# FNet with a gated linear unit: neighbouring tokens share a partition, the normalising passes walk in storage order, and the first DFT block is loaded in one piece

## The chip, the cores and the metric

One core of a Trainium2 chip runs the whole kernel. The metric is the device time of one execution in microseconds; the time before is the median of three runs. The trace and the page of the profile come from one profiled execution of the same kernel.

## The reference

All values are 32-bit floats, S = 2048 tokens, D = 512 features, F = 1792.

```python
xn = layernorm(x)                       # over the 512 features of a token
a, b = xn @ Wd_re.T, xn @ Wd_im.T       # DFT along the features
s = Ws_re @ a - Ws_im @ b               # DFT along the tokens, real part
h = sigmoid(xn @ w_gate) * (xn @ w_up)
g = silu(h @ w_down)
out = x + s * g
```

## The kernel before

**Work and engines.** The kernel does the DFT along the tokens first, then the gated unit on the transposed x, then the DFT along the features. Each matrix product is cut into 2 by 2 blocks and done with seven block products instead of eight (Strassen's scheme in Winograd's form), so VectorE forms sums of blocks (`combine`, L127), and every operand is split into a high and a low part for three passes of TensorE: ScalarE writes the high part (L118), VectorE the low one by a subtraction (L123), TensorE multiplies (`mm3`, L70). GpSimd issues the stores to scratch memory (g_part, f_raw, f_sum) and does small arithmetic of the statistics; SyncE issues all loads.

**Order.** The program is written as a list of units, each one block product, with 12 to 18 matmuls. A loop at the end (L851) goes through the units, and ahead of each one loads what the next five need, splits what the next two need, and runs what was hung on that unit with `sooner`, `amid` and `after`. No scheduler moves anything: the instructions of an engine run in the order in which this loop emits them.

**Tokens.** Tokens are cut into 4 groups of 512 (index pp or b), and each group into 4 blocks of 128 tokens, named by (e, j). Block halves j = 0 and 1 are the two halves of the 2 by 2 scheme along the tokens; e counts the two 128-row pieces that a page holds. Before, token 128 (4 pp + 2 e + j) + p lies on partition p. The page `xs[j, pp]` is [128, 2, 512]; `fetch` (L149) fills it with two transfers of 128 rows each. `seq` in `_layout` lays the two DFT matrices out on the host in the matching order, in blocks [128, 2, 512], each contiguous in memory. `c_block` names such a block, and `Load.load` (L76) fetches it with one transfer.

**Statistics.** `stats` (L156) forms mean, scale and bias of each token with VectorE (L162, L163, L168, L170) and GpSimd (L169, L171) into the tile `moments`. `normalise` (L174) applies them on ScalarE, a token for each partition. `store_moments` writes mean and scale of a group to scratch memory as m_part, [128, 2, 4].

**The normalising passes by features.** For the gated unit, x is needed with features on partitions: `x_t` holds it transposed, a page [128 features, 2, 512 tokens], tokens in their order in memory. Here mean and scale differ along the row, so `x_norm` (L425) loads m_part to every partition as `both`, [128, 128 p, 2, 4], and `step` (L431) adds the mean in one pass and multiplies by the scale in the next, in place, each one VectorE instruction over 128x1024 (L435). There are 16: 2 halves, 2 groups in each, 2 pages, 2 passes. They are hung on units at the end of the DFT along the tokens and within the gated unit.

**The startup.** `begin` (L347) warms TensorE with products of ones, then emits the first loads by hand: the two pieces of the first x page, the two halves of the first DFT block (L358), and then x pages and DFT blocks by turns. The first unit's operands are split by halves e, the DFT block's half ahead of x's (`high` L376, `low` L379, `normed` L373).

Of the kernel before, what the change touches and what calls it, by code (L numbers as in the profile page):

```python
# [8 lines left out]
F32 = mybir.dt.float32  # L9
F32R = mybir.dt.float32r  # L10
AF = mybir.ActivationFunctionType
# [3 lines left out]
P = 128  # L15
# [6 lines left out]
NT = S // 512  # L22
SB = 512
# [9 lines left out]
def fnet_glu_kernel(ctx: ExitStack, tc: tile.TileContext, x, x_t, c_re, c_im, w_h, w_gu, w_down, out):  # L33
    nc = tc.nc
# [8 lines left out]
    def page(shape, dtype=F32R):  # L43
        return pages.tile([P, *shape], dtype, name="page")

    def bank(tag):
        return banks.tile([P, 512], F32, name=tag, bufs=2 if tag == "pd" else 1)
# [7 lines left out]
    moments = const.tile([P, 4, 3, 2, 2], F32, name="moments")  # L55
    m_part = [dram.tile([P, 2, 4], F32, name=f"m_part{i}") for i in range(NT)]
# [42 lines left out]
    class Parts(Value):  # L99
# [6 lines left out]
        def begin(self):  # L106
            if self.raw is None and self.at is None:
                self.raw = self.src()
# [21 lines left out]
    units = []  # L130
# [6 lines left out]
    def after(n, f):  # L137
        extra.setdefault(n, []).append(f)

    def sooner(n, f):  # L140
        early.setdefault(n, []).append(f)
# [5 lines left out]
    xs, mvs = {}, {}  # L147

    def fetch(j, pp, es=(0, 1)):  # L149
        if (j, pp) not in xs:  # L150
            xs[j, pp] = page([2, D], F32)
        for e in es:
            i = 4 * pp + 2 * e + j
            nc.sync.dma_start(xs[j, pp][:, e, :], x[i * P : (i + 1) * P, :])

    def stats(j, pp):  # L156
        mv = stat.tile([P, 2, 2], F32, name="mv")
        rs = stat.tile([P, 2], F32, name="rs")
        mean, scale, bias = (moments[:, pp, m, :, j] for m in range(3))
        for e in range(2):  # L160
            st = stat.tile([P, 6], F32, name="st")
            nc.vector.bn_stats(st, xs[j, pp][:, e, :])  # L162
            nc.vector.bn_aggr(mv[:, e, :], st)  # L163
            if pp == j == 0:
                nc.gpsimd.tensor_scalar(rs[:, e : e + 1], mv[:, e, 1:2], EPS, None, op0=ALU.add)
                nc.gpsimd.tensor_tensor(scale[:, e : e + 1], rs[:, e : e + 1], mhalf[:, e : e + 1], op=ALU.pow)
        if pp or j:
            nc.vector.tensor_scalar(rs, mv[:, :, 1], EPS, None, op0=ALU.add)  # L168
            nc.gpsimd.tensor_tensor(scale, rs, mhalf, op=ALU.pow)  # L169
        nc.vector.tensor_scalar(mean, mv[:, :, 0], -1.0, None, op0=ALU.mult)  # L170
        nc.gpsimd.tensor_tensor(bias, mean, scale, op=ALU.mult)  # L171
        return mv

    def normalise(j, pp, d=None):  # L174
        for e in range(2):
            v = xs[j, pp][:, e, :] if d is None else a_block(d, j, pp)[:, e]
            nc.scalar.activation(v, v, AF.Identity, scale=moments[:, pp, 1, e, j : j + 1], bias=moments[:, pp, 2, e, j : j + 1])

    def store_moments(b):
        nc.gpsimd.dma_start(m_part[b], moments[:, b, 0:2].rearrange("p m e j -> p m (e j)"))  # L180


    def a_block(d, j, pp):
        return xs[j, pp][:, :, d * D // 2 : (d + 1) * D // 2]
# [130 lines left out]
    def begin_seq():  # L315
        tags = ("a", "b", "pd"), ("c", "pd", "a"), ("b", "pd", "a"), ("c", "a", "pd")
        chunks = [Chunk(t, dict(zip("abc", tags[t])), t in (1, 2)) for t in range(NT)]
        for i, k in enumerate((1, 2)):
            for pp in range(4):
                for c in chunks[:2]:  # L320
                    add(c.needs(k, pp), lambda c=c, k=k, pp=pp: c.run(k, pp))
                m = 8 * i + 2 * pp
                if m > 4:
                    sooner(m - (6, 7)[i], lambda i=i, pp=pp: fetch(i, pp))
                if m > 2:
                    sooner(m - (4, 5)[i], lambda i=i, pp=pp: stats(i, pp))
                    sooner(m - 2, units[m][0][1].get)
                    sooner(m - 2, lambda i=i, pp=pp: normalise(i, pp))
                if i:
                    after(m + 2, lambda pp=pp: store_moments(pp))  # L330
# [16 lines left out]
    def begin(chunks):  # L347
        for i, tag in enumerate(("gb", "ub", "pd", "pd")):
            idle = bank(tag)
            for _ in range((4, 4, 2, 2)[i]):  # L350
                nc.tensor.matmul(idle, ones[:, :P], ones, start=True, stop=True)
        c = chunks[0].op[1, 0]
        raw = c.loads[0]
        raw.at = page(raw.shape, F32)
        for e in range(2):
            fetch(0, 0, (e,))
        for e in range(2):
            nc.sync.dma_start(raw.at[:, e, :], raw.src[:, e, :])  # L358
        fetch(0, 1)
        for n in (1, 2):  # L360
            units[n][0][1].load()
        fetch(0, 2)
        for n in (3, 4, 5):
            units[n][0][1].load()
        a = aop[1, 0]
        both = page([2, 2, D // 2])
        a.at = both[:, 0], both[:, 1]
        c.at = page([2, SB]), page([2, SB])
        first = a_block(0, 0, 0)

        def normed(e):
            scale = moments[:, 0, 1, e, 0:1]
            nc.vector.tensor_scalar(first[:, e], first[:, e], mv[:, e, 0:1], scale, op0=SUB, op1=ALU.mult)  # L373

        def high(parts, src, e):
            nc.scalar.activation(parts[0][:, e], src[:, e], AF.Copy)  # L376

        def low(parts, src, e):
            nc.vector.tensor_tensor(parts[1][:, e], src[:, e], parts[0][:, e].bitcast(F32), op=SUB)  # L379

        mv = stats(0, 0)
        high(c.at, raw.at, 0)
        normed(0)
        high(a.at, first, 0)
        low(c.at, raw.at, 0)
        low(a.at, first, 0)
        high(c.at, raw.at, 1)
        normed(1)
        high(a.at, first, 1)
        low(c.at, raw.at, 1)  # L390
        low(a.at, first, 1)
        units[1][0][1].high()
        stats(0, 1)
        units[1][0][1].get()
        units[2][0][1].get()
        normalise(0, 1, d=0)
        aop[1, 1].get()
        for pp in range(2):
            after(4 + pp, lambda pp=pp: normalise(0, pp, d=1))
# [25 lines left out]
    def x_norm(h, b, at):  # L425

        c = 2 * h + b
        both = Load(m_part[c].rearrange("p m o -> (p m o)").partition_broadcast(P).rearrange("k (p m o) -> k p m o", m=2, o=4), [P, 2, 4])
        raw = [Load(x_t[c * 2 + j], [2, SB]) for j in range(2)]

        def step(j, m):  # L431
            v = xraw[h, j, b] = raw[j].load()
            to = v.rearrange("k i (o p) -> k i o p", o=4)
            by = both.load()[:, :, m, :].rearrange("k p o -> k o p").unsqueeze(1).to_broadcast([P, 2, 4, P])
            nc.vector.tensor_tensor(to, to, by, op=(ADD, ALU.mult)[m])  # L435

        sooner(at[0] - 5, both.load)
        for i in range(4):
            if i % 2 == 0:
                sooner(at[i] - 5, raw[i // 2].load)  # L440
            after(at[i], lambda i=i: step(*divmod(i, 2)))
# [381 lines left out]
    with tc.manual_schedule():  # L823
        chunks = begin_seq()
        n = len(units)
# [48 lines left out]
def _layout(inputs):  # L874
    import numpy as np

    def seq(c):
        c = np.asarray(c).reshape(NT, SB, 4, 2, 2, P)
        return np.ascontiguousarray(c.transpose(0, 4, 2, 5, 3, 1))

    def hid(re, im):
        w = np.stack([np.asarray(v).T.reshape(2, 2, P, 2, D // 2) for v in (im, re)])
        return np.ascontiguousarray(w.transpose(4, 1, 3, 0, 2, 5)).reshape(2, 2, P, 4, D // 2)

    def quads():
        a = np.stack([np.asarray(inputs["B_w_gate"]), np.asarray(inputs["B_w_up"])])
        a = a.reshape(2, 2, 2, P, NG, 2, P)
        a = a.transpose(4, 5, 1, 3, 0, 2, 6)
        order = [[(0, 0), (0, 1)], [(1, 1), (1, 0)]]
        return np.ascontiguousarray(  # L890
            np.stack([np.stack([a[:, i, j] for i, j in k], axis=2) for k in order], axis=1)
        ).reshape(NG, 2, P, 2, 4 * P)

    return {
        "x": np.ascontiguousarray(np.asarray(inputs["A_x"]).reshape(S, D)),
        "x_t": np.ascontiguousarray(
            np.asarray(inputs["A_x"]).reshape(NT, SB, 2, 2, P).transpose(0, 2, 4, 3, 1)
        ).reshape(2 * NT, P, 2, SB),
        "c_re": seq(inputs["A_dft_seq_re"]),
        "c_im": seq(inputs["A_dft_seq_im"]),  # L900
        "w_h": hid(inputs["A_dft_hid_re"], inputs["A_dft_hid_im"]),
        "w_gu": quads(),
        "w_down": np.ascontiguousarray(np.asarray(inputs["B_w_down"]).reshape(NG, 2, P, D).transpose(0, 2, 1, 3)),
    }
# [16 lines left out]
```

## Time and profile before

| | us |
|---|---|
| median of 3 runs (809.91 to 810.92) | 810.75 |
| the profiled execution | 810.13 |
| its span | 808.3 |
| TensorE busy | 789.9 (98%) |
| VectorE busy | 699.5 (87%) |
| ScalarE busy | 510.6 (63%) |
| GpSimd busy | 122.2 (15%) |

The clock granted to TensorE is 0.999 of the full one over the span. The DMA engines move 174.72 MB, 216 GB/s on the mean. In rows of the profile PE is TensorE's matrix work, PEld its loading of weights, DVE VectorE, ACT ScalarE, POOL GpSimd and SP SyncE; L435 is line 435 of the kernel before; `x16 | 34.2, 2138 | 0.0` reads: 16 instructions, 34.2 us busy, 2138 ns each, 0.0 us idle of the engine ahead of them. A row of the timeline gives start, length, engine, line, operation, and in brackets the idle time ahead and who ended it.

### The profile page before, as it was taken

What the parts mean: (1) busy time and instruction counts of PE and PEld (TensorE: products, weight loads), DVE (VectorE), ACT (ScalarE), POOL (GpSimd) and SP (SyncE); (2) the same over time, 40 slices, a digit from 0 to 9 for tenths busy, and PEclk for the clock granted to TensorE, in tenths of its full rate; (3) what the DMA queues carried; (4) which work ended last, traced back from release to release, by engine and by line L of the source; (5) the groups of instructions that cost most, each with busy time, mean ns of one, the idle gap of its engine ahead of it and who ended that gap; (6) DMA issues with size and microseconds to landing.
All of it is one profiled execution on the core that took longest, in us unless ns stands there. A gap on an engine that the chain in (4) does not pass through costs nothing.

```text
span 808.3 us, 9885 instructions
## 1 busy us (share of the span) xinstructions
PE 789.9 (98%) x3468; PEld 649.1 (80%) x3468; DVE 699.5 (87%) x894; ACT 510.6 (63%) x776; POOL 122.2 (15%) x162
## 2 busy tenths in 40 slices
PE   7999999999999999999998999999999999999997
PEld 5788888888878888878876887888888888888886
DVE  7898999788899999899999966869688888896957
ACT  4984654534434455676767866767577787897571
POOL 3330001001110000011211211222131121111301
PEclk9999999999999999999999999999999999999999
DMA  9964066385997336137965987799999798999996
GB/s 347 405 210 156 1 212 230 128 340 217 295 415 298 104 131 212 50 126 198 214 115 82 171 168 179 237 272 247 259 234 221 160 232 223 230 286 305 301 332 105
DMA packets 50481, 174.72 MB, mean 216 GB/s; under 512 B 5632, under 2 KB 5888, under 8 KB 50432
## 3 DMA queue, kind: packets, MB, share of 16 engines
q0 software_dynamic: 20320, 70.28, 39.6%
q1 hardware_dynamic: 30032, 103.76, 35.6%
q8 instruction: 27, 0.44, 0.2%
q14 instruction: 22, 0.18, 0.1%
q10 hardware_dynamic: 80, 0.07, 0.0%
HBM read 106.95 MB, written 70.80 MB: 220 GB/s over the span
## 4 chain that ended last, share of the span: by engine, by line
PE 59%; issue 27%; DMA 6%; DVE 4%; POOL 3%; ACT 1%; SPq 0%; POOLq 0%; DVEq 0%; ACTq 0%
PE pd L70 18%; PE ga L70 11%; PE ua L70 11%; PE uc L70 6%; PE gc L70 6%; DMA g_part<-page 4%; PE ub L70 4%; PE gb L70 4%; POOL g_part L477 2%; DVE page L127 1%; DVE page L123 1%; DMA f_raw<-page 1%; DMA page<-in_c_re_dram 1%; DVE st L162 0%; POOL f_raw L273 0%
## 5 line engine op out<-in xcount | busy, mean ns | idle before, releaser
L118 ACT ACTIVATE page<-page 128x512 fp32r<-128x512 f32 (+1 forms) x384 | 303.6, 831 | 159.8 <-DVE page L127 131.7
L123 DVE TENSOR_TENSOR page<-page 128x512 fp32r<-128x512 f32 (+1 forms) x384 | 349.3, 941 | 59.2 <-ACT page L118 57.2
L70 PE MATMUL pd<-page 128*128 128x512 f32 (+1 forms) x984 | 238.9, 387 | 1.8 <-ACT page L486 1.1
L70 PEld LDWEIGHTS pd<-page 128*128 128x128 f32 x984 | 182.9, 188 | 40.7 <-ACT page L486 1.5
L127 DVE TENSOR_TENSOR page<-page 128x1024 f32<-128x1024 f32 (+2 forms) x252 | 205.5, 836 | 3.5 <-DMA page<-in_w_gu_dram 2.7
L70 PE MATMUL ga<-page 128*128 128x512 f32 x600 | 154.2, 391 | 6.9 <-ACT page L118 2.9
L70 PE MATMUL ua<-page 128*128 128x512 f32 x600 | 153.0, 389 | 0.0
L70 PEld LDWEIGHTS ga<-page 128*128 128x128 f32 x600 | 112.1, 188 | 33.4 <-ACT page L594 4.9
L70 PEld LDWEIGHTS ua<-page 128*128 128x128 f32 x600 | 112.6, 188 | 23.5
L477 POOL DMA_DIRECT2D g_part<-page x76 | 66.4, 874 | 281.1 <-ACT page L486 160.7
L70 PE MATMUL gc<-page 128*128 128x512 f32 x384 | 98.9, 390 | 0.4 <-DVE page L123 0.3
L70 PE MATMUL uc<-page 128*128 128x512 f32 x384 | 98.4, 389 | 0.0
L486 ACT ACTIVATE page<-pd 128x512 f32<-128x512 f32 x140 | 81.4, 599 | 23.4 <-PE pd L70 16.1
L70 PEld LDWEIGHTS gc<-page 128*128 128x128 f32 x384 | 71.8, 188 | 16.3 <-DVE page L123 0.9
L70 PEld LDWEIGHTS uc<-page 128*128 128x128 f32 x384 | 72.1, 188 | 15.0
L70 PE MATMUL gb<-page 128*128 128x512 f32 x252 | 64.9, 390 | 2.0 <-DVE page L123 2.0
L70 PE MATMUL ub<-page 128*128 128x512 f32 x252 | 64.6, 389 | 0.0
L70 PEld LDWEIGHTS gb<-page 128*128 128x128 f32 x252 | 47.2, 188 | 12.2 <-DVE page L123 2.4
L70 PEld LDWEIGHTS ub<-page 128*128 128x128 f32 x252 | 47.3, 188 | 9.8
L273 POOL DMA_DIRECT2D f_raw<-page x16 | 8.7, 545 | 220.0 <-DVE page L285 147.1
L435 DVE TENSOR_TENSOR page<-page 128x1024 f32<-128x1024 f32 x16 | 34.2, 2138 | 0.0
L612 DVE TENSOR_TENSOR page<-page 128x512 f32<-128x512 f32 x28 | 19.3, 690 | 8.0 <-ACT page L609 7.1
(90 smaller groups left out, 344.4 us busy)
## 6 DMA issues: line engine op xcount, KB each, us to landing
g_part<-page POOLq DMA_DIRECT2D x84, 512.0 KB, 7.1
page<-in_c_re_dram SPq DMA_DIRECT2D x47, 512.0 KB, 7.1
page<-in_c_im_dram SPq DMA_DIRECT2D x32, 512.0 KB, 6.1
page<-f_raw SPq DMA_DIRECT2D x28, 512.0 KB, 7.7
page<-in_w_gu_dram SPq DMA_DIRECT2D x22, 512.0 KB, 6.4
f_raw<-page POOLq DMA_DIRECT2D x16, 512.0 KB, 6.2
f_sum<-page POOLq DMA_DIRECT2D x16, 512.0 KB, 7.4
page<-f_sum SPq DMA_DIRECT2D x16, 512.0 KB, 12.2
```

What stands on the lines that cost most here:

```text
L70: nc.tensor.matmul(ps, ws[w], ms[m], start=first and i == 0, stop=last and i == 2, skip_group_check=go_on)
L118: nc.scalar.activation(self.parts[0], self.raw, AF.Copy)
L123: nc.vector.tensor_tensor(lo, self.raw, hi.bitcast(F32), op=SUB)
L127: (engine or nc.vector).tensor_tensor(dst, a, b, op=op)
L273: nc.gpsimd.dma_start(f_raw[self.t][block], v)
L435: nc.vector.tensor_tensor(to, to, by, op=(ADD, ALU.mult)[m])
L477: nc.gpsimd.dma_start(g_part[i], pg, accum_op=ADD)
L486: nc.scalar.activation(pg[:, o, :], po, AF.Copy, scale=float(sign))
L612: nc.vector.tensor_mul(s[k][:, 0, :], s[k][:, 0, :], ps["u" + tag] if tag else s[k][:, 1, :])
```

## The change

Token 512 pp + 4 p + 2 j + e now lies on partition p. So a page `xs[j, pp]` takes two neighbouring rows of x for each partition, and `fetch` of a whole page is one transfer of 4 KB pieces; the first page is still fetched as two transfers, of 2 KB pieces with a step of 8 KB. `seq` lays the DFT matrices out to match, `moments` has its last two indices exchanged. In `step` the token index of a row of 512 is now 4 p + (2 j + e), so both operands are walked with the four values of a partition p innermost, which is the order in which `both` stores them: four neighbouring floats, then a gap of four to the next p. Before, p was the innermost index, with a step of 8 floats in `both`. The number, shape and place of all passes stay as they are.

In `begin`, the first DFT block is fetched by one transfer. The second unit's block goes ahead of the second x page, and one more block ahead of the third.

```diff
     def fetch(j, pp, es=(0, 1)):
         if (j, pp) not in xs:
             xs[j, pp] = page([2, D], F32)
-        for e in es:
-            i = 4 * pp + 2 * e + j
-            nc.sync.dma_start(xs[j, pp][:, e, :], x[i * P : (i + 1) * P, :])
+        rows = x[pp * SB : (pp + 1) * SB, :].rearrange("(p j e) d -> p j e d", j=2, e=2)[:, j]
+        if len(es) == 2:
+            nc.sync.dma_start(xs[j, pp], rows)
+        else:
+            nc.sync.dma_start(xs[j, pp][:, es[0], :], rows[:, es[0], :])
...
-        mean, scale, bias = (moments[:, pp, m, :, j] for m in range(3))
+        mean, scale, bias = (moments[:, pp, m, j, :] for m in range(3))
...
         c = chunks[0].op[1, 0]
         raw = c.loads[0]
-        raw.at = page(raw.shape, F32)
         for e in range(2):
             fetch(0, 0, (e,))
-        for e in range(2):
-            nc.sync.dma_start(raw.at[:, e, :], raw.src[:, e, :])
+        raw.load()
+        for n in (1,):
+            units[n][0][1].load()
         fetch(0, 1)
-        for n in (1, 2):
+        for n in (2, 3):
             units[n][0][1].load()
         fetch(0, 2)
-        for n in (3, 4, 5):
+        for n in (4, 5):
             units[n][0][1].load()
...
         def step(j, m):
             v = xraw[h, j, b] = raw[j].load()
-            to = v.rearrange("k i (o p) -> k i o p", o=4)
-            by = both.load()[:, :, m, :].rearrange("k p o -> k o p").unsqueeze(1).to_broadcast([P, 2, 4, P])
+            to = v.rearrange("k i (p o) -> k i p o", o=4)
+            by = both.load()[:, :, m, :].unsqueeze(1).to_broadcast([P, 2, P, 4])
             nc.vector.tensor_tensor(to, to, by, op=(ADD, ALU.mult)[m])
...
     def seq(c):
-        c = np.asarray(c).reshape(NT, SB, 4, 2, 2, P)
-        return np.ascontiguousarray(c.transpose(0, 4, 2, 5, 3, 1))
+        c = np.asarray(c).reshape(NT, SB, 4, P, 2, 2)
+        return np.ascontiguousarray(c.transpose(0, 4, 2, 3, 5, 1))
```

Two lines are added within `fetch`, so that lines behind it have numbers greater by two in the changed kernel: L435 there is L437, L376 is L378. Elsewhere in the code `normalise`, `store_moments` and `normed` follow the exchanged indices of `moments`.

The order of SyncE's queue at the program's start, before (in_x_dram is x, in_c_re_dram the real DFT matrix, one row of 128x512 is 256 KB):

```order
L154 DMA page<-in_x_dram 128x512 x2
L358 DMA page<-in_c_re_dram 128x512 x2
L154 DMA page<-in_x_dram 128x512 x2
L79 DMA page<-in_c_re_dram 128x1024 x2
L154 DMA page<-in_x_dram 128x512 x2
L79 DMA page<-in_c_re_dram 128x1024 x3
L154 DMA page<-in_x_dram 128x512 x4
```

and the same piece in the changed kernel:

```order
L156 DMA page<-in_x_dram 128x512 x2
L79 DMA page<-in_c_re_dram 128x1024 x2
L154 DMA page<-in_x_dram 128x1024
L79 DMA page<-in_c_re_dram 128x1024 x2
L154 DMA page<-in_x_dram 128x1024
L79 DMA page<-in_c_re_dram 128x1024 x2
L154 DMA page<-in_x_dram 128x1024 x2
```

The first DFT block and the first unit's counterpart for the second chunk now stand ahead of the second x page; each x page from there on is one transfer, and one DFT block has moved ahead of the third.

ScalarE at the program's start, before, with the semaphores that each instruction waits for (DMAHW2 and so on are lanes of SyncE's transfers, used by turns; L376 splits the first unit's operands, L118 is the next block's high part):

```order
L376 ACTIVATE page<-page 128x512 [waits DMAHW2_49]
L376 ACTIVATE page<-page 128x256 [waits DMAHW0_49,DVE_49]
L376 ACTIVATE page<-page 128x512 [waits DMAHW3_49]
L376 ACTIVATE page<-page 128x256 [waits DMAHW1_49,DVE_49]
L118 ACTIVATE page<-page 128x1024 [waits DMAHW6_49]
```

and in the changed kernel:

```order
L378 ACTIVATE page<-page 128x512 [waits DMAHW2_49]
L378 ACTIVATE page<-page 128x256 [waits DMAHW0_49,DVE_49]
L378 ACTIVATE page<-page 128x512
L378 ACTIVATE page<-page 128x256 [waits DMAHW1_49,DVE_49]
L118 ACTIVATE page<-page 128x1024 [waits DMAHW3_49]
```

The third instruction has lost its wait, since the first one's transfer brings both halves, and the second block's high part waits for the transfer right behind it. The order of instructions on ScalarE, VectorE, TensorE and GpSimd is the same in both kernels.

More of the change, by code (lines that the diff above doesn't have):

```diff
@@ L176, in normalise @@
             v = xs[j, pp][:, e, :] if d is None else a_block(d, j, pp)[:, e]
-            nc.scalar.activation(v, v, AF.Identity, scale=moments[:, pp, 1, e, j : j + 1], bias=moments[:, pp, 2, e, j : j + 1])
+            nc.scalar.activation(v, v, AF.Identity, scale=moments[:, pp, 1, j, e : e + 1], bias=moments[:, pp, 2, j, e : e + 1])
     def store_moments(b):
-        nc.gpsimd.dma_start(m_part[b], moments[:, b, 0:2].rearrange("p m e j -> p m (e j)"))
+        nc.gpsimd.dma_start(m_part[b], moments[:, b, 0:2].rearrange("p m j e -> p m (j e)"))
     def a_block(d, j, pp):
@@ L371, in normed @@
         def normed(e):
-            scale = moments[:, 0, 1, e, 0:1]
+            scale = moments[:, 0, 1, 0, e : e + 1]
             nc.vector.tensor_scalar(first[:, e], first[:, e], mv[:, e, 0:1], scale, op0=SUB, op1=ALU.mult)
```

## The prediction

> **What bounds the kernel now.** I read the page first, then TensorE's waits, then VectorE in the stretches where those waits stand. The page's line of engines:
>
> ```profile
> PE 789.9 (98%) x3468; PEld 649.1 (80%) x3468; DVE 699.5 (87%) x894; ACT 510.6 (63%) x776; POOL 122.2 (15%) x162
> ```
>
> TensorE is busy for 98% of the span, and the change gives it the same instructions. What can move is only the time it loses, and the waits of TensorE list it; behind the startup they lie in 200 to 300 and in 340 to 460 us, but for one (columns: total us, times, longest):
>
> ```profile
> PE gb L70 <- DVE page L123: 2.0, 1, 2.0
> PE gc L70 <- DVE page L123: 0.3, 1, 0.3
> ```
> ```profile
> PE ga L70 <- ACT page L594: 2.0, 3, 0.7
> PE pd L70 <- ACT page L486: 1.1, 1, 1.1
> PE pd L70 <- DVE page L572: 0.7, 1, 0.7
> ```
>
> The first group (2.3 us) names VectorE, the second (3.8 us) VectorE or ScalarE. That VectorE is the real cause there shows in the busy times by stretch (columns: length, then PE, PEld, DVE, ACT, POOL):
>
> ```profile
> 218.80:236.70 17.90, 15.89 (x71) 12.81 (x70) 17.90 (x17) 4.79 (x6) 2.87 (x5) 1.00 1.00 379
> 236.70:274.00 37.30, 37.02 (x162) 30.32 (x163) 37.25 (x29) 17.23 (x20) 2.34 (x4) 1.00 0.60 243
> 340.00:400.00 60.00, 59.43 (x262) 48.65 (x261) 58.50 (x86) 45.49 (x81) 8.27 (x11) 1.00 0.65 169
> 400.00:460.00 60.00, 56.77 (x246) 45.34 (x245) 59.45 (x82) 42.87 (x75) 10.40 (x12) 1.00 0.71 114
> ```
>
> VectorE is full: 17.90 of 17.90 us, 37.25 of 37.30, 59.45 of 60. So in these stretches, and only there, a shorter VectorE instruction is a shorter kernel. What a wait costs beyond its idle time is seen around the one at 432.62 on TensorE's timeline:
>
> ```profile
> 429.98 1.52 PE L70 MATMUL uc<-page 128*128 128x512 f32 x6
> 432.62 1.66 PE L70 MATMUL pd<-page 128*128 128x512 f32 x6 [1.12 <-ACT page L486]
> 434.12 1.52 PE L70 MATMUL gb<-page 128*128 128x512 f32 x6
> 435.48 0.84 PE L70 MATMUL ub<-page 128*128 128x512 f32 x3
> ```
>
> Undisturbed, six matmuls start 1.36 us after the six before (434.12 to 435.48). Here the steps are 2.64 and 1.50, so 1.42 us are lost where the row says 1.12: 0.30 more for each wait. The first group thus loses 2.3 + 2 x 0.3 = 2.9 us, the second 3.8 + 5 x 0.3 = 5.3 us, and 8.2 us in all is the most that a faster VectorE can return here.
>
> **The normalising passes (L435).** The groups by shape:
>
> ```profile
> L127 DVE TENSOR_TENSOR page<-page 128x1024 f32<-128x1024 f32 x92 | 112.0, 1224 | 0.0
> ...
> L435 DVE TENSOR_TENSOR page<-page 128x1024 f32<-128x1024 f32 x16 | 34.2, 2138 | 0.0
> ```
>
> Same operation, same shape, same type, yet 2138 ns against 1224. The difference is how the second operand is walked: `both` is [token p, mean or scale, 4], and the old order takes p innermost, a step of 8 floats at every element. The new order takes the 4 neighbouring floats first and hops after each four. No row of this trace walks an operand so. The bounds are 1224 (as L127, no hop) and 2138 (a hop as dear as four old steps). If a hop costs what it costs now, (2138 - 1224) / 1024 = 0.89 ns, 256 of them add 0.23 us and the pass takes 1.45. I take the end that it is nearest to, 1.22 us, so 0.9 us less for each pass, 14.6 us of VectorE's time over 16.
>
> [...]
>
> Where the passes lie decides what they are worth. The busy time of L435 alone, in the stretches between TensorE's waits:
>
> ```profile
> 216.80:236.70 19.90, 4.28 (x2) 1.00 1.00 382
> 236.70:270.00 33.30, 8.59 (x4) 1.00 0.62 254
> 340.00:354.00 14.00, 2.10 (x1) 1.00 0.10 39
> 354.00:400.00 46.00, 6.45 (x3) 1.00 0.82 208
> 400.00:422.00 22.00, 8.57 (x4) 1.00 0.72 129
> ```
>
> The waits stand at:
>
> ```profile
> 236.68 1.43 PE L70 MATMUL gb<-page 128*128 128x512 f32 x5 [2.01 <-DVE page L123]
> 269.92 1.43 PE L70 MATMUL gc<-page 128*128 128x512 f32 x5 [0.28 <-DVE page L123]
> ```
> ```profile
> 353.60 1.65 PE L70 MATMUL ga<-page 128*128 128x512 f32 x6 [0.57 <-ACT page L594]
> ```
> ```profile
> 412.13 1.65 PE L70 MATMUL ga<-page 128*128 128x512 f32 x6 [0.68 <-ACT page L594]
> ```
>
> The other three of the second group come after 412.13, the first of them at 432.62 (above). One by one: ahead of 236.68 two passes save 1.8 us of the 2.3 lost there; 0.5 stays. Four more lie ahead of 269.92, where 0.6 is lost, and all of it goes. One lies ahead of 353.60 (4 us earlier), and its 0.9 covers the 0.9 lost. Three passes up to 400 us I count at nothing: VectorE has 1.5 us of idle time in 340 to 400, so it was not the limit all along, and TensorE lost nothing between. Four lie in 400 to 422, behind which 3.8 - 0.57 = 3.2 us of idle time and 4 x 0.3 are lost, 4.4 in all; they save 3.6, and VectorE stays the limit for the remaining 0.8. ScalarE, which the rows name here, waits for VectorE itself and follows it. Sum: 1.8 + 0.6 + 0.9 + 3.6 = **6.9 us gained**.
>
> **The first block whole, and the new order of loads.** The chain of work through the startup:
>
> ```profile
> 1.65 4.17 DMA page<-in_c_re_dram
> 5.82 0.02 issue
> 5.84 0.64 ACT page L376
> ...
> 8.79 0.61 DVE st L162
> ...
> 15.51 0.61 DVE st L162
> ```
>
> ScalarE's first split starts when the first half of the block is in, at 5.82. Now it waits for both halves. SyncE's timeline has the issues of the halves and of the next block, and the DMA issues of two narrow windows how long the second half and that next block took to land:
>
> ```profile
> 1.65 0.91 SPq L358 DMA_DIRECT2D page<-in_c_re_dram  x2
> ...
> 3.55 0.91 SPq L79 DMA_DIRECT2D page<-in_c_re_dram  x2
> ```
> ```profile
> page<-in_c_re_dram SPq DMA_DIRECT2D x1, 256.0 KB, 4.4
> ```
> ```profile
> page<-in_c_re_dram SPq DMA_DIRECT2D x1, 512.0 KB, 5.6
> ```
>
> The second half, issued at some 2.1 (0.91 us for both), was in at 2.1 + 4.4 = 6.5, 0.7 us behind the first. The one transfer needs one issue instead of two, so I take 0.6 us of delay; the ends are 0 (in as soon as the half was) and 0.7. Everything on the chain follows from this split, by ScalarE's and VectorE's order, up to TensorE's last wait of the startup:
>
> ```profile
> 21.98 1.20 PE L70 MATMUL ga<-page 128*128 128x512 f32 x4 [1.41 <-ACT page L118]
> ```
>
> The next wait in its timeline is that at 236.68, so nothing in between takes a delay up. **0.6 us lost**, in full.
>
> The x load that L162 waits for moves behind a 512 KB block. The bytes up to and with it are the same as were up to and with that block, which was in at 3.55 + 5.6 = 9.15. VectorE comes to L162 at 8.79 + 0.6 = 9.4, so the move costs nothing by 0.25 us; should the slower split not come, this cover is gone and 0.35 is the price. Behind it come two blocks and the next x load, 1.5 MB; at the rate of the 2 MB moved from 1.65 to 9.15 these take 5.6 us and are in by 14.8, and L162 asks for that x at 15.51 + 0.6 = 16.1. SP's queue issues seven transfers fewer and is not the limit. Longer pieces of x and moments stored side by side I cost at nothing: neither shortens the chain above.
>
> **Sum.** 6.9 - 0.6 = 6.3 us less. The profiled execution took 810.13 us (span 808.3, 1.8 around it) and would take 803.8. The runs' median, 810.75, is 0.6 above it, so 810.75 - 6.3 = 804.45, rounded **804.5 us**.
>
> **Rivals.**
> - *B, the freed time is only half returned.* In 400 to 460 us ScalarE stands between VectorE and every wait, with 42.87 us of work in its own order. If its order holds, only the waits that name VectorE or have a pass right ahead (1.8 + 0.6 + 0.9) go, and little behind 400: 3.3 - 0.6 = 2.7 less, 808.1; with 0.7 lost at the start and the 0.6 at 269.92 not returned, 808.8. For it: the 0.8 that is left anyway. Against it: VectorE at 59.45 of 60.
> - *C, the passes stay at 2.1 us.* The change of order would then not do what it seems to, because the broadcast, not the step, is what costs. That leaves the 0.6 lost: 811.4, within 0.2% (1.6 us, about what a measurement of this kernel can tell from no change). Against it: the broadcast re-reads rows, and costs no fetch that L127 doesn't make too. [...]
> - *D, slower: short runs are dearer than single steps.* Each pass restarts its walk 256 times. Over 914 / 256 = 3.6 ns a restart, the pass gets slower. At twice that, it takes 3.05 us, the same seven passes ahead of the waits push TensorE back by 7 x 0.9 = 6.3 us, and with the startup that is 817.7. Against it: a hop at every element costs 0.89 ns now.
>
> **Chances and range.** The forecast 0.68, B 0.18, C 0.08, D 0.06. Faster by over 0.2%: the forecast and nearly all of B, 0.84; within 0.2%: C and the tail of B, 0.10; slower: D, 0.06. The range goes from all 8.2 us returned with no loss at the start (802.5) to B's far end (808.8); C and D, 0.14, and what little lies past the ends are left out.
>
> **What would show it.** L435's line (two lines further down in the changed file) at about 1.2 us and x16. TensorE's wait near 236 down from 2.0 to some 0.3, the one near 270 gone, at most one left of those from 412 to 444. The one wait of TensorE behind 460 us unchanged, as no pass lies near it. The first split some 0.6 us later than 5.84, TensorE's first real matmul and its last wait of the startup by as much. I am wrong if the passes stay above 1.5 us, if VectorE gets idle time in 400 to 460 and TensorE still waits there, or if the startup's waits grow by over a microsecond.

## The result, and the profile after

| | median us | lowest to highest | ratio to before | 95% interval |
|---|---|---|---|---|
| before (5 runs) | 810.6 | 808.49 to 810.92 | | |
| changed (5 runs) | 803.86 | 802.95 to 804.23 | 0.9921 | 0.9909 to 0.9933 |

The changed kernel is 6.7 us faster by the medians. Its profiled execution took 804.23 us with a span of 802.4, 5.9 us less than that of before; the traces are compared on this difference. The ranges of the two kernels do not meet.

The passes, in the groups by shape of the changed kernel (L437 is the former L435):

```profile
L127 DVE TENSOR_TENSOR page<-page 128x1024 f32<-128x1024 f32 x92 | 111.5, 1218 | 0.2 <-DMA page<-in_c_im_dram 0.2
...
L437 DVE TENSOR_TENSOR page<-page 128x1024 f32<-128x1024 f32 x16 | 19.5, 1217 | 0.0
```

A pass now costs what the other operations of its shape cost, 1217 ns instead of 2138: 14.7 us of VectorE's time are gone. TensorE's waits behind the startup, for 200 to 300, 340 to 460 and 460 to 800 us:

```profile
PE gb L70 <- DVE page L123: 0.4, 1, 0.4
```
```profile
PE ga L70 <- ACT page L596: 0.5, 1, 0.5
```
```profile
PE ga L70 <- ACT page L596: 0.6, 1, 0.6
```

Of 2.3 us of waits in the first stretch 0.4 are left, of 3.8 in the second 0.5. VectorE by stretch:

```profile
340.00:400.00 60.00, 60.00 (x266) 49.63 (x266) 56.47 (x87) 45.91 (x81) 9.14 (x12) 1.00 0.69 175
400.00:460.00 60.00, 59.51 (x263) 48.96 (x262) 59.45 (x87) 47.36 (x81) 10.37 (x12) 1.00 0.76 133
```

In 400 to 460 us VectorE is as full as it was (59.45), but it does 87 instructions there instead of 82, and TensorE 263 instead of 246. The startup went the other way. VectorE's first statistics, ScalarE's first split and TensorE's first real matmul, before and changed (brackets: the idle time ahead and what ended it):

```profile
3.41 0.69 DVE L162 BATCH_NORM_STATS2 st<-page 128x6 f32<-128x512 f32 x1 [2.02 <-DMA page<-in_x_dram]
...
6.83 1.26 PE L70 MATMUL ga<-page 128*128 128x512 f32 x3 [1.05 <-ACT page L376]
```
```profile
4.14 0.70 DVE L164 BATCH_NORM_STATS2 st<-page 128x6 f32<-128x512 f32 x1 [2.75 <-DMA page<-in_x_dram]
...
6.05 0.69 DVE L164 BATCH_NORM_STATS2 st<-page 128x6 f32<-128x512 f32 x1 [1.00 <-DMA page<-in_x_dram]
...
7.37 1.46 ACT L378 ACTIVATE page<-page 128x512 fp32r<-128x512 f32 x3 [5.14 <-DMA page<-in_c_re_dram]
...
8.35 1.29 PE L70 MATMUL ga<-page 128*128 128x512 f32 x3 [1.42 <-ACT page L378]
```

The split, at 7.37, starts 1.53 us later than before (5.84), not 0.6, and the x pieces, whose landing I took as unchanged, are late too: the second one at 6.05, where VectorE before never waited for it.

Since TensorE does the same matmuls in the same order in both, the time of the n-th one in the two traces shows where time went. The delay of the changed kernel is +1.52 us at the first real matmul, +1.75 behind the last wait of the startup (21.98 before), +1.71 ahead of the wait near 236 us, and -6.08 at the end of the last wait (502.78 before). Behind that it changes by no more than 0.05 us. By place:

| place (time before, us) | predicted, us | measured, us |
|---|---|---|
| startup | +0.6 | +1.71 |
| wait at 236.68 | -1.8 | -1.64 |
| wait at 269.92 | -0.6 | -0.43 |
| wait at 353.60 | -0.9 | -0.74 |
| waits from 410 to 444 | -3.6 | -3.95 |
| smaller losses near 292, 382, 496 and 502 | 0 | -1.03 |
| sum | -6.3 | -6.08 |

### The profile page after: what moved, and what is told of

Read it like the earlier page. It is cut to its first block, busy times and chain, and to the rows that moved or that the text cites. A ratio compares the mean times of both kernels' runs of the same rounds, so it can differ in the third digit from the quotient of the medians.

```text
span 802.4 us, 9870 instructions
## 1 busy us (share of the span) xinstructions
PE 790.3 (98%) x3468; PEld 651.6 (81%) x3468; DVE 685.9 (85%) x894; ACT 510.7 (64%) x776; POOL 123.0 (15%) x162
## 4 chain that ended last, share of the span: by engine, by line
PE 85%; DVE 5%; DMA 4%; issue 4%; POOL 1%; ACT 1%; SPq 0%; POOLq 0%; ACTq 0%; DVEq 0%
PE pd L70 25%; PE ga L70 15%; PE ua L70 15%; PE gc L70 10%; PE uc L70 10%; PE gb L70 5%; PE ub L70 5%; DMA g_part<-page 2%; DVE page L127 2%; DVE page L123 1%; DMA page<-in_x_dram 1%; DMA f_raw<-page 1%; POOL g_part L479 1%; ACT page L118 0%; DVE page L574 0%
## 5 line engine op out<-in xcount | busy, mean ns | idle before, releaser
L118 ACT ACTIVATE page<-page 128x512 fp32r<-128x512 f32 (+1 forms) x384 | 303.1, 829 | 148.3 <-DVE page L127 116.5
L574 DVE TENSOR_TENSOR page<-page,pd 128x512 f32<-128x512 f32 x28 | 18.5, 684 | 6.9 <-PE pd L70 6.9
```

The lines of the kernel that those rows point to most:

```text
L118: nc.scalar.activation(self.parts[0], self.raw, AF.Copy)
L574: nc.vector.tensor_add(self.part[:, o, :], self.part[:, o, :], ps)
```

## The experiments

My theory: a single-float step of 32 bytes in the second operand is what costs 0.9 us a pass; where VectorE is full, its time shows one for one at TensorE; the whole block delays the first split by 0.6 to 0.7 us. What was open after the result was the other 1.1 us of the startup. The theories are numbered in the expectation of the first run. All ratios are to the kernel before, on the same chip.

**The startup's loads alone, on the kernel before.** Edit:

```diff
-        raw.at = page(raw.shape, F32)
         for e in range(2):
             fetch(0, 0, (e,))
-        for e in range(2):
-            nc.sync.dma_start(raw.at[:, e, :], raw.src[:, e, :])
+        raw.load()
+        for n in (1,):
+            units[n][0][1].load()
         fetch(0, 1)
-        for n in (1, 2):
+        for n in (2, 3):
...
```

> The kernel before with the startup's part of the change alone: first DFT block in one transfer and the changed order of loads; tokens, x pieces and passes as before. Theory 1 (the whole block is what delays the first split): the split starts at 6.4 to 6.6 us instead of 5.84, the first real matmul 0.6 us later, the kernel 0.6 us slower (ratio 1.0007). Theory 2 (the x pieces of 2 KB with a step of 8 KB are what made the changed kernel's startup later than that): the same 0.6 us here, and the other 1.1 us of the changed kernel's 1.7 are missing. Theory 3 (the order and the single transfer cost all of it): split at 7.3 us, 1.7 us slower (ratio 1.002). Passes at 2.14 us in all three.

Measured: 811.02 us against 810.46, ratio 1.0004 (0.9993 to 1.0014), which by itself tells nothing apart. The trace does:

```profile
3.23 0.69 DVE L162 BATCH_NORM_STATS2 st<-page 128x6 f32<-128x512 f32 x1 [1.84 <-DMA page<-in_x_dram]
...
6.61 1.46 ACT L376 ACTIVATE page<-page 128x512 fp32r<-128x512 f32 x3 [4.39 <-DMA page<-in_c_re_dram]
...
7.59 1.26 PE L70 MATMUL ga<-page 128*128 128x512 f32 x3 [0.66 <-ACT page L376]
```

The first x piece lands as early as before (3.23 against 3.41), and the split starts at 6.61, 0.77 us behind 5.84; TensorE's first real matmul is 0.76 late, and the matmul behind its second wait (at 14.84 before) 0.75. So the block in one piece, with the new order of loads, costs 0.7 to 0.8 us, as theory 1 had it, and theory 3 falls. The run does not separate the single transfer from the 512 KB block that is now issued right behind it. Half of the changed kernel's delay is still missing here.

**The step of the x pieces alone, on the kernel before.** Edit:

```diff
             i = 4 * pp + 2 * e + j
-            nc.sync.dma_start(xs[j, pp][:, e, :], x[i * P : (i + 1) * P, :])
+            rows = x[i * P : (i + 1) * P, :]
+            if pp == j == 0:
+                rows = x[:SB, :].rearrange("(p r) d -> p r d", r=4)[:, e, :]
+            nc.sync.dma_start(xs[j, pp][:, e, :], rows)
```

> The kernel before, but the first x page's two pieces are read from rows with a step of 8 KB in place of neighbouring rows (so these 256 rows of x are other tokens' values, and the result differs); nothing else changed. Theory (the step of the pieces delays their landing, as in the changed kernel): they land at 4.1 to 4.8 and 5.3 to 6.1 us instead of 3.4 and 4.1, the first DFT half behind them 0.5 us or more later than 5.82, the first real matmul 0.5 to 0.8 us later, the kernel 0 to 0.8 us slower (ratio 1.000 to 1.001). Rival (the late landing came from something else in the new layout, or by chance): 3.2 to 3.4 and 4.1 to 4.3 us, ratio 1.000.

Measured: 810.31 us against 810.02, ratio 1.0006 (0.9996 to 1.0016). The trace:

```profile
4.89 0.69 DVE L165 BATCH_NORM_STATS2 st<-page 128x6 f32<-128x512 f32 x1 [3.50 <-DMA page<-in_x_dram]
...
6.15 0.63 ACT L379 ACTIVATE page<-page 128x512 fp32r<-128x512 f32 x1 [3.92 <-DMA page<-in_c_re_dram]
...
7.73 0.98 PE L70 MATMUL ga<-page 128*128 128x512 f32 x3 [1.63 <-ACT page L379]
```

As many 2 KB pieces as before, at the same place in the queue, only 8 KB apart in memory instead of adjacent: VectorE starts on them 1.5 us later (4.89 against 3.41), and TensorE's first real matmul is 0.90 late, the one behind its second wait 0.72. The first DFT half, queued behind them, is late by 0.3, less than the 0.5 that I had expected. So the step is most of the missing part, and it is no chance of one run: in the traces of the seven kernels that have it VectorE's statistics wait 3.4 to 3.9 us in sum for x, in the three without it 2.0. The two edits together, 0.75 + 0.72 us at the second wait, make up 1.47 of the changed kernel's 1.70 there; at the first split they make up less, 0.77 + 0.31 = 1.08 of 1.53. What is left is not settled; the second x page, which the new order puts behind a block, ends VectorE's wait at 10.41 where VectorE was free at 10.36, so it has little part in it.

**The changed kernel with the old loads.** The inverse of the first edit, on the changed kernel: first block in halves, old order, new tokens and passes.

> The changed kernel with the startup's loads as before: first block in halves, old order; tokens and passes as changed. Theory 1 and 3: split back near 5.84 us, passes 1.22 us, the kernel 7.8 us faster than before (802.8, ratio 0.990), 1.0 to 1.7 us faster than the changed one. Theory 2: the first x pieces still land late (4.1 and 6.0 us instead of 3.4 and 4.1), the split starts 0.5 us or more behind 5.84, and the kernel gains 0.6 us or less on the changed one.

Measured: 801.79 us against 810.46, ratio 0.9897 (0.9882 to 0.9913), the fastest of all the kernels that were run, 2 us below the changed one (the intervals overlap by a little). Its start:

```profile
4.74 0.69 DVE L164 BATCH_NORM_STATS2 st<-page 128x6 f32<-128x512 f32 x1 [3.35 <-DMA page<-in_x_dram]
...
5.97 0.63 ACT L378 ACTIVATE page<-page 128x512 fp32r<-128x512 f32 x1 [3.75 <-DMA page<-in_c_re_dram]
...
7.58 1.00 PE L70 MATMUL ga<-page 128*128 128x512 f32 x3 [1.64 <-ACT page L378]
```

The split is back at 5.97, and x is late (4.74), as theory 2 has it for x and theory 1 for the block. But the matmul behind TensorE's second wait, 0.46 us *earlier* than before although the first one is 0.75 later, was in nobody's theory. The trace points at GpSimd: its power for the statistics (it raises the variance to -1/2), which stands on the startup's chain, took 0.70 us here and 1.68 before. VectorE's next split and this power, before, then this kernel:

```profile
10.59 1.22 DVE L123 TENSOR_TENSOR page<-page 128x1024 fp32r<-128x1024 f32 x1
10.69 1.68 POOL L169 TENSOR_TENSOR moments<-rs,mhalf 128x2 f32<-128x2 f32 x1 [4.23 <-DVE moments L170]
```
```profile
11.17 0.70 POOL L171 TENSOR_TENSOR moments<-rs,mhalf 128x2 f32<-128x2 f32 x1 [3.11 <-DVE moments L172]
11.25 1.23 DVE L123 TENSOR_TENSOR page<-page 128x1024 fp32r<-128x1024 f32 x1
```

Before, the split had started 0.10 us ahead of the power; here it started 0.08 us behind it. That became a theory of its own, tested next.

**A small delay on VectorE.** On the kernel with the old loads, in `stats`:

```diff
-        nc.vector.tensor_scalar(mean, mv[:, :, 0], -1.0, None, op0=ALU.mult)
+        for _ in range(3 if pp or j else 1):
+            nc.vector.tensor_scalar(mean, mv[:, :, 0], -1.0, None, op0=ALU.mult)
```

> The changed kernel with the old order of loads and the block in halves, and in the statistics (all but the first) VectorE's small product with -1 done three times over, 0.2 to 0.4 us of delay ahead of the next split. Theory (GpSimd's power takes 1.68 us when VectorE's next large operation has begun before it and 0.70 when not): the power takes 0.6 to 0.8 us everywhere, and each of the two that stand on the startup's chain saves 1 us less the delay: 0.5 to 1.5 us faster than without the delay (800.3 to 801.3, ratio 0.988 to 0.989). Rival (it is slow for another reason): powers at 1.68 us still, and 0.2 to 0.8 us slower (802.0 to 802.6).

Measured: 802.36 us against 810.02, ratio 0.9913 (0.9900 to 0.9927). The mechanism is as expected. The power before (seven instructions), then with the delay:

```profile
L169 POOL TENSOR_TENSOR moments<-rs,mhalf 128x2 f32<-128x2 f32 x7 | 9.7, 1389 | 22.0 <-DVE moments L170 22.0
```
```profile
L171 POOL TENSOR_TENSOR moments<-rs,mhalf 128x2 f32<-128x2 f32 x7 | 4.9, 693 | 23.3 <-DVE moments L173 23.3
```

All seven take 0.69 us on the mean, and TensorE's last old startup wait ends 0.73 us earlier than before. The time, though, is no better than without the delay: a new wait has come, and by it the advantage is gone (the 90th matmul starts when it did before).

```profile
26.49 0.73 PE L70 MATMUL gc<-page 128*128 128x512 f32 x2 [0.38 <-DVE page L123]
```

VectorE, late by the repeated small products, is now what TensorE waits for. For GpSimd's power 0.1 us of order decides: in the traces of before and of the changed kernel it took 1.66 to 1.68 us the eleven times that VectorE's 128x1024 split had begun 0.10 to 0.11 us ahead of it, and 0.69 the three times that VectorE's next split came 0.29 to 0.41 us behind. For VectorE's split the order decides nothing: begun 0.08 us behind the power it took 1.23 us, begun ahead 1.22. Why the power takes longer is not shown.

**The first x page in one transfer.** On the kernel with the old loads, `for e in range(2): fetch(0, 0, (e,))` becomes `fetch(0, 0)`.

> The changed kernel with the old order of loads and the block in halves, and the first x page in one transfer of 4 KB pieces with a step of 8 KB. If it is many small pieces at that step that land late: the page is in by 4.6 us, ahead of the second piece's 5.33, and the kernel 0.5 us faster than with two pieces (801.3). If the step itself is slow: the page is in at 5.3 us or later, the statistics of the first piece start 0.6 us later, and the kernel is 0 to 0.6 us slower than with two pieces (801.8 to 802.4).

Measured: 803.41 us, ratio 0.9919 (0.9906 to 0.9933).

```profile
5.10 0.69 DVE L164 BATCH_NORM_STATS2 st<-page 128x6 f32<-128x512 f32 x1 [3.71 <-DMA page<-in_x_dram]
```

The whole page is in at 5.1, neither the 4.6 of the first case nor the 5.3 of the second, and in time the kernel is worse than the second case allowed (803.4 for 801.8 to 802.4): the statistics start 0.36 us later than with two pieces, and the power fell back to 1.67 us. Larger pieces do not buy back the step. Why a step of 8 KB delays these first transfers is open.

**Mean and scale turned in memory, old tokens.** On the kernel before, m_part is stored as [mean or scale, block, token], so that the passes walk it without a step:

```diff
...
-        nc.gpsimd.dma_start(m_part[b], moments[:, b, 0:2].rearrange("p m e j -> p m (e j)"))
+        nc.gpsimd.dma_start(m_part[b].rearrange("m o p -> p m o"), moments[:, b, 0:2].rearrange("p m e j -> p m (e j)"))
...
-            by = both.load()[:, :, m, :].rearrange("k p o -> k o p").unsqueeze(1).to_broadcast([P, 2, 4, P])
+            by = both.load()[:, m].unsqueeze(1).to_broadcast([P, 2, 4, P])
```

> The kernel before, with mean and scale stored as [mean or scale, block, token] so that the passes walk them with no step, in the old token order; loads as before. Theory (the step of 8 floats costs the 0.9 us, not the token order and not the broadcast): passes 1.22 us, waits of TensorE at 236 to 0.4 us, at 270, 353 and 412 to 442 gone, the kernel 7.8 us faster (802.8, ratio 0.990). Rival (the broadcast or the token order costs it): passes at 2.14 us, ratio 1.000.

Measured: 806.11 us against 810.46, ratio 0.9943 (0.9925 to 0.9961). The passes are as expected, in the old token order:

```profile
L435 DVE TENSOR_TENSOR page<-page 128x1024 f32<-128x1024 f32 x16 | 19.5, 1217 | 0.0
```

So it is the step, and neither the broadcast nor the token order. The time is 3.3 us over what I expected. One of its six runs took 802.23 us, what I had expected, and the others 805.22 to 806.91, so what costs the time does not come in every execution; the trace is of one of the longer ones (806.88). In it TensorE has a new wait of 2.4 us, near 85 us, followed by some 3 us at a lower granted clock (0.55, the third number from the end), over 130 us ahead of the first pass:

```profile
PE pd L70 <- DVE page L123: 2.4, 1, 2.4
```
```profile
86.00:89.20 3.20, 3.20 (x10) 2.48 (x9) 3.20 (x4) 1.88 (x4) 0.00 (x0) 0.55 0.37 150
```

The store of m_part now goes out in 4-byte pieces. DMA issues of 43 to 59 us, before, then this kernel (last number: us to landing):

```profile
page<-in_c_im_dram SPq DMA_DIRECT2D x4, 512.0 KB, 5.8
page<-in_c_re_dram SPq DMA_DIRECT2D x2, 512.0 KB, 4.0
f_raw<-page POOLq DMA_DIRECT2D x2, 512.0 KB, 6.8
m_part<-moments POOLq DMA_DIRECT2D x4, 4.0 KB, 4.8
```
```profile
page<-in_c_im_dram SPq DMA_DIRECT2D x4, 512.0 KB, 18.2
page<-in_c_re_dram SPq DMA_DIRECT2D x2, 512.0 KB, 10.7
f_raw<-page POOLq DMA_DIRECT2D x2, 512.0 KB, 21.6
m_part<-moments POOLq DMA_DIRECT2D x4, 4.0 KB, 16.0
```

In this trace four stores of 4 KB hold up half-megabyte transfers by 7 to 15 us. Compared matmul by matmul, 5.2 us were lost up to there, 4.4 of them at the new wait and just behind it, and from the wait at 236 on 8.3 us won. That the late transfers are what TensorE's wait near 85 goes back to is inferred from their place, not shown. The changed kernel's token order buys the same passes without this store.

**Single floats with a step of two.** On the changed kernel, m_part is stored as [token, 4, mean or scale], with two small stores in place of one, so that a pass takes single floats 8 bytes apart. The question is whether the passes need the runs of four neighbouring floats of the changed kernel, or whether a shorter step of single floats is enough. Edit:

```diff
...
-        nc.gpsimd.dma_start(m_part[b], moments[:, b, 0:2].rearrange("p m j e -> p m (j e)"))
+        for m in range(2):
+            nc.gpsimd.dma_start(m_part[b][:, :, m], moments[:, b, m].rearrange("p j e -> p (j e)"))
...
-            by = both.load()[:, :, m, :].unsqueeze(1).to_broadcast([P, 2, P, 4])
+            by = both.load()[:, :, :, m].unsqueeze(1).to_broadcast([P, 2, P, 4])
```

> [...]

Measured: 807.06 us, ratio 0.9961 (0.9949 to 0.9973), 3.2 us over the changed kernel's 803.86, with the same trouble from 4-byte stores as in the run before (from 60 to 104 us TensorE loses 3.2 us). On the passes the answer is clear:

```profile
L438 DVE TENSOR_TENSOR page<-page 128x1024 f32<-128x1024 f32 x16 | 19.5, 1217 | 0.0
```

No two floats of this walk are neighbours, and the pass takes 1217 ns all the same, so the runs of four of the changed kernel are not needed for it. Four walks of the second operand were run: single floats 32 bytes apart (before) take 2138 ns; single floats 8 bytes apart, runs of four with a gap of four, and a walk with no step take 1217 each. At which step between 8 and 32 bytes single floats become slow, and why, is not shown.

**Half of the passes slow again.** On the changed kernel, the passes of the second half of the tokens walk with the token innermost (the lines follow those that set `to` and `by`):

```diff
+            if h:
+                to = v.rearrange("k i (p o) -> k i o p", o=4)
+                by = both.load()[:, :, m, :].rearrange("k p o -> k o p").unsqueeze(1).to_broadcast([P, 2, 4, P])
```

> The changed kernel, but the 8 passes of the second half of the tokens (350 to 420 us) walk with the token innermost again: step of 8 floats in mean and scale, step of 4 in x, read and written. Theory (VectorE sets the pace there, so what these passes take shows one for one): passes of the first half 1.22 us, of the second 2.1 to 3.1; TensorE's time up to 340 us as in the changed kernel, and the 5.5 us won behind it gone, 809 to 810 us at 2.1 us a pass, more by up to 5 us at 3.1 (ratio 0.998 to 1.005). Rival (the freed time there is only partly returned, ScalarE's order holds): under 3 us lost against the changed kernel, 804 to 807.

Measured: 809.86 us against 810.02, ratio 0.9999 (0.9990 to 1.0008). The passes' busy time in the two halves:

```profile
216.00:300.00 84.00, 9.76 (x8) 1.00 0.65 248
340.00:430.00 90.00, 18.11 (x8) 1.00 0.68 154
```

1.22 us each in the first half, 2.26 in the second. TensorE's waits in 200 to 300 us stay short, those in 340 to 460 are back:

```profile
PE gb L70 <- DVE page L123: 0.2, 1, 0.2
```
```profile
PE ga L70 <- ACT page L599: 2.2, 3, 0.8
PE pd L70 <- ACT page L491: 1.1, 1, 1.1
PE pd L70 <- DVE page L577: 0.9, 2, 0.7
```

Compared matmul by matmul, this kernel is 0.86 us ahead of before near 292 us and 0.47 at 503; the changed one goes from 0.56 to 6.08. So undoing eight passes takes back all that was won up to 450 us, with the 2.26 us that they take in place of the 2.14 of before, and the rival, that ScalarE's order would keep much of it from TensorE, is refuted.

## Why the prediction was right

804.5 us was forecast and 803.86 measured.

**The passes: right.** 1217 ns against the 1.22 us taken; the end of the bounds that was chosen is the one that came.

**What they return: right in mechanism and place, a little too small in sum (6.9 us forecast, 7.2 measured where it can be the passes, and 0.6 more that slow passes win too).** The wait at 236 came down to 0.38 (0.3 forecast), that at 270 went, one of those from 412 to 444 is left. The kernels with quick passes agree: from the wait at 236 on, the changed one wins 7.8 us, the one with the old loads 7.8, the one with the delay 7.9, the one with the first x page whole 7.8. Four quicker passes free 3.7 us, and 3.95 came back from 410 to 444, so the three passes before 400 that I counted at nothing probably gave some of it. What I left at zero are the smaller losses near 292, 382, 496 and 502, 1.0 us together; the last of these I had called unchanged for having no pass near it, and it was shorter (1.05 to 0.78 us lost at its first matmul). Not all of the 1.0 can be laid to the passes: the kernel before with the new loads alone, its passes slow, also wins 0.52 us near 496 and 502, and the one with half of the passes slow 0.48, against 0.57 in the changed kernel. Why is open.

**Rival B: refuted** by the run with half of the passes slow; that the rows named ScalarE meant only that ScalarE waited for VectorE. **Rivals C and D: refuted** by the passes' length, here and in the old token order. D's price was too low by its own logic: it counted seven passes and left out the other four ahead of 269.92, where VectorE was as full.

**The startup: the term that was mis-sized.** Forecast 0.6, bounds 0 to 0.7; measured 1.71, more than the microsecond that the prediction named as a sign of being wrong. The part that I reasoned about, waiting for the whole block, is 0.75. The step that failed is the sentence that costs the x pieces at nothing. It weighed the 4 KB pieces of later pages and not the first page's 2 KB pieces, which the change moves 8 KB apart; that costs 0.7 by itself, and 0.2 of the sum are not settled. The new place of the second x page cost 0.05 instead of nothing. SyncE's queue issues eight transfers fewer (seven of x, one of the first block), not seven, and nothing hung on that. The lost clock, in the windows of the changed kernel's startup, cost next to nothing:

```profile
18.00:21.00 3.00, 3.00 (x9) 2.32 (x8) 2.93 (x7) 0.39 (x1) 1.81 (x2) 0.51 1.03 421
```

TensorE ran at half its clock (0.51) for three microseconds behind its wait at 16.54, and fell 1.6 us further behind; but the next wait of before, at 21.98, belongs to the chain of the statistics through VectorE, GpSimd and ScalarE, and the half-speed matmuls only filled it.

The two errors, 1.1 us too little lost and 0.9 too little won, nearly cancelled, and over half of the second is not shown to come from the passes. That the sum is within 1 us of the runs is in part luck.

## What to carry to other kernels

Look in the groups by shape for one operation that takes longer than its equals: a walk with a wide step through one operand made it 2138 ns instead of 1217 here. The cure may be a different assignment of rows to partitions, which here cost 0.7 us through the first loads, rather than a transposing store, which here cost some 5 us in the execution that was traced. The worth of a shorter instruction is read from the stretches where its engine has no idle time and another engine waits, nearly one for one there and little elsewhere: 3.95 us came back here for the 3.7 freed from 400 to 422, and 7.8 at most of the 14.7 freed in all. When a layout changes, cost every transfer whose pieces it moves apart, the first ones of the program above all, since nothing runs ahead of them.

## What the runs showed of the hardware

- With four stores of 4 KB in 4-byte pieces, 512 KB transfers issued beside and behind them took 11 to 22 us to land instead of 4 to 7; with eight such stores of 2 KB, in the run with a step of two, 10 to 22.
- 2 KB pieces with a step of 8 KB, as the first transfers of the program, were used 1.5 us later than adjacent ones (4.89 against 3.41 at VectorE), and 0.7 later in the changed kernel (4.14). The reason is open.
- GpSimd's operation on two elements took 0.69 or 1.68 us, by whether VectorE's next 128x1024 split began 0.1 us ahead of it; the split took 1.22 to 1.23 us either way.
- TensorE's granted clock was 0.51 for some 3 us after a wait of 1.78 us in the changed kernel, and the second four matmuls behind that wait took 1.71 us. After waits at the same place of 1.52 us before (clock 1.00), of 1.77 in the run of the startup's loads alone and of 1.78 in the one with the first x page whole, the same four took 0.91 to 0.92, so the length of that wait alone does not decide it.
